# A fused attention and expert-mixture kernel: stores of the last first-layer tiles on another queue, three experts' second-layer weights loaded later, loads and preparations in another order

## The chip, the cores and the metric

The kernel runs on one core of a Trainium2 chip. The metric is the device time of one execution in microseconds (us). TensorE multiplies matrices, VectorE and ScalarE work element by element, GpSimd and SyncE here mostly issue DMAs. Each of ScalarE, SyncE and GpSimd has a DMA queue of its own. An engine takes its instructions strictly in the order of the program, and a DMA issue is such an instruction, waits included. The chip's profiler records one execution; its page calls the engines PE, DVE, ACT, POOL and SP.

## The reference

The first half is attention over 8 batches and 8 heads with 512 local tokens (a window of 32 to each side) and 32 global tokens. Its result, as a matrix `x` of 4352 tokens by 512, feeds a mixture of 8 experts whose routing weights come from 8 rounds of row and column scaling:

```python
logits = x @ w_gate
P = np.exp(logits - logits.max())
for _ in range(8):
    P /= P.sum(1, keepdims=True) + 1e-09
    P /= P.sum(0, keepdims=True) + 1e-09
    P *= N / E
for e in range(E):
    h = np.maximum(x @ w1[e], 0.0)
    out += P[:, e:e + 1] * (h @ w2[e])
```

## The kernel before

**Groups, fillers, units.** The tokens are cut into 9 groups `m`: eight of 512 local tokens and a last one (`m = 8`) of the 256 global tokens. The first layer of experts 0 to 3 needs no routing weight, so it is computed early, as filler work between the steps of the attention: filler (e, m) is `p_l1`, eight tiles `fm` of four matmuls (L466), each followed by a relu (L469 on ScalarE, L471 on VectorE) into a tile `hT`, and after the eighth a store of the whole tile to DRAM (`hd[e][m]`, L473). Fillers run in the order (0,0), (1,0), (2,0), (3,0), (0,1) and so on. The fillers left over when the attention is done are run by `tail_run` (L869), which hands `p_l1` its PSUM pool in the argument `pool`; the fillers within the attention don't set that argument. `tail_run` is called between the steps of the routing rounds (L880 to L888) and once more for all that is left (L901).

**The second stage** runs over 72 units, group by group, with the experts of a group in the order `ORDER = (4, 0, 5, 1, 6, 2, 7, 3)`. Even units are experts 4 to 7: the group's `x` is loaded (`load_x`), scaled by the routing weight (`scale_x`, with the weights `pb` from `load_pb`, which spreads a row of 512 over 128 partitions), and multiplied by first-layer weights `w1s` (`load_w1`, 1 MB; `l1`, L736, relu L738 into `h`). Odd units are experts 0 to 3: their `h` is loaded back from DRAM (`load_h`, L722, 1 MB) and scaled (`scale_h`). Then both go through the second layer as a two-by-two block product with seven products instead of eight (`product`, L779): `sums` makes the sums and differences of blocks of `h`, `prep_w2c` those of the weights `w2c[e]`, five VectorE instructions an expert, once. `add` (L795, L793) brings products from PSUM to the output tile, `store` and, for the last unit, `last_pair` (L819) write it out.

**What sets the order.** The program is scheduled by hand, in the order of the text. Tiles with few buffers tie the engines together: `hT` and `h` share 4 buffers, `w1s` has 2 (the fillers' weights of experts 0 and 1 sit in them first), `pb`, `xs` and `xg` have 2 each, and `ps_rot`, the PSUM tiles of `l1` and of products 6 and 7, has 3. One turn of the loop at L918 does one unit; an even turn `i` holds the first layer of unit `i + 2` among the products of unit `i`, an odd turn has products alone. A pair is an even and an odd turn. SyncE issues, in the order of the program: the stores of fillers; `load_pb(0)`, `load_x(0)`, `load_w1(0)`, `load_pb(1)`, `load_pb(2)` (L890 to L895); the stores of the fillers of L901; `load_w1(2)`, `load_h(1)`; and then in each even turn two `load_pb`, now and then `load_x`, `load_h(i+3)` and `load_w1(i+4)` (L923 to L928). GpSimd issues the second-layer weights, four DMAs an expert (`load_w2c`, L668), which also turn them from 32 to 16 bits: six experts at L682 and the last two, 7 and 3, at L905 to L907, in memory that `xT` has left.

Of the kernel before, what the change touches and what calls it, by code (L numbers as in the profile page):

```python
# [9 lines left out]
FP16 = mybir.dt.float16  # L10
# [13 lines left out]
def kernel(  # L24
# [13 lines left out]
    nc = tc.nc  # L38

    B, H, Sl, Dh = q_l.shape  # L40
# [3 lines left out]
    P = 128  # L44
# [8 lines left out]
    FT = F // P  # L53
# [20 lines left out]
    hd = [[ydram.tile([P, FT, n], FP16, name=f"hd{e}_{m}") for m, (_, n) in enumerate(groups)] for e in range(NL)]  # L74
# [15 lines left out]
    with tc.tile_pool(name="att_c", bufs=1) as att_c, \  # L90
# [131 lines left out]
        for i in range(2):  # L222
            for f, src, eng in zip(f0, (q_l, k_l), (nc.scalar, nc.sync)):
                eng.dma_start(out=f[:, 2 * i : 2 * i + 2].rearrange("p h s d -> p h (s d)"),
                              in_=src[0, 2 * i : 2 * i + 2].rearrange("h (p s) d -> p h (s d)", s=NJ))
# [26 lines left out]
        for so in range(NJ):  # L252
            for c0, n in ((W, P), (W + Sl, W // NJ)):
                nc.vector.tensor_copy(out=zsel[:, so, c0 : c0 + NJ * n].rearrange("p (x s) -> p x s", s=NJ)[:, :, so],
                                      in_=identity[:, 0:n])
# [201 lines left out]
        hTs, wts = {}, {}  # L457

        def p_l1(e, m, fm, eng, pool=None, tag="mm"):
            n = groups[m][1]  # L460
            if fm == 0:
                hTs[(e, m)] = hpool.tile([P, FT, 512], FP16, tag="hT", name="hT")
            hT = hTs[(e, m)]
            ph = (pool or ps_mm).tile([P, 512], FP32, tag=tag, name="ph")
            for dk in range(DP):
                nc.tensor.matmul(ph[:, 0:n], wts[e][:, dk, P * fm : P * (fm + 1)], xT[m][:, dk, :],  # L466
                                 start=(dk == 0), stop=(dk == DP - 1))
            if eng == "a":
                nc.scalar.activation(out=hT[:, fm, 0:n], in_=ph[:, 0:n], func=AF.Relu)  # L469
            else:  # L470
                nc.vector.tensor_scalar(out=hT[:, fm, 0:n], in0=ph[:, 0:n], scalar1=0.0, scalar2=None, op0=ALU.max)  # L471
            if fm == FT - 1:
                nc.sync.dma_start(out=hd[e][m], in_=hT[:, :, 0:n])  # L473

        def load_w1e(e):
            pool, kw = ((wpool, dict(tag="w1e")), (wpool, dict(tag="w1e")), (wpool, dict(tag="w2e", bufs=1)),
# [96 lines left out]
        for s in range(HP, NU + 1):  # L573
            slot = s
            b, hp = divmod(s, HP)
# [84 lines left out]
    ORDER = (4, 0, 5, 1, 6, 2, 7, 3)  # L660
# [4 lines left out]
    def load_w2c(e):  # L665
        w = w2c[e]
        for i, (f, d) in ((1, (0, 0)), (4, (1, 1)), (2, (0, 1)), (3, (1, 0))):
            nc.gpsimd.dma_start(out=w[:, i], in_=moe_w2[e][P * HF * f : P * HF * (f + 1), HD * d : HD * (d + 1)]  # L668
                                .rearrange("(fko fki) d -> fki fko d", fki=P))
# [4 lines left out]
    def prep_w2c(e):  # L674
        w = w2c[e]
        tt(w[:, 0], w[:, 1], w[:, 4], ALU.add)
        tt(w[:, 5], w[:, 1], w[:, 2], ALU.add)
        tt(w[:, 6], w[:, 3], w[:, 4], ALU.add)
        tt(w[:, 2], w[:, 2], w[:, 4], ALU.subtract)
        tt(w[:, 3], w[:, 3], w[:, 1], ALU.subtract)  # L680

    for e in ORDER[:6]:  # L682
        load_w2c(e)

    units = [(m, e) for m in range(B + 1) for e in ORDER]
# [3 lines left out]
    def load_w1(i):  # L689
        if i < NUN:  # L690
            w1s[i] = wpool.tile([P, DP, F], FP16, tag="w1e", name="w1s")
            nc.sync.dma_start(out=w1s[i], in_=w1d[units[i][1] - NL])

    def load_pb(i):
        if i < NUN:
            m, e = units[i]
            c0, n = groups[m]
            pbs[i] = xsp.tile([P, 512], FP32, tag="pb", name="pb")
            nc.sync.dma_start(out=pbs[i][:, 0:n], in_=pd[e, c0 : c0 + n].partition_broadcast(P))
# [6 lines left out]
    def scale_x(i):  # L706
        if i < NUN:
            m = units[i][0]
            n = groups[m][1]
            xss[i] = xsp.tile([P, DP, 512], FP16, tag="xs", name="xs")  # L710
            tt(xss[i][:, :, 0:n], xgs[m][:, :, 0:n],
               pbs.pop(i)[:, 0:n].unsqueeze(1).to_broadcast([P, DP, n]), ALU.mult)
# [17 lines left out]
    def l1(i, fm, pool, tag):  # L730
        if i >= NUN:
            return
        n = groups[units[i][0]][1]
        ph = pool.tile([P, 512], FP32, tag=tag, name="ph")
        for dk in range(DP):
            nc.tensor.matmul(ph[:, 0:n], w1s[i][:, dk, P * fm : P * (fm + 1)], xss[i][:, dk, 0:n],  # L736
                             start=(dk == 0), stop=(dk == DP - 1))
        nc.scalar.activation(out=hs[i][:, fm, 0:n], in_=ph[:, 0:n], func=AF.Relu)  # L738

    def sums(i):  # L740
        if i >= NUN - 1:
            return
        n = groups[units[i][0]][1]
        t1, t2 = slice(0, n // 2), slice(n // 2, n)
        h = hs[i]
        s = ss[i] = (wpool.tile([P, 3, HF, 256], FP16, tag="w2e", name="s", bufs=1) if i % 2 else
                     wr.tile([P, 3, HF, 256], FP16, tag="s", name="s"))
        lo, hi = h[:, 0:HF], h[:, HF:FT]
        tt(s[:, 0:2, :, 0 : n // 2], lo[:, :, 0:n].rearrange("p k (a t) -> p a k t", a=2),
           hi[:, :, 0:n].rearrange("p k (a t) -> p a k t", a=2), ALU.add)  # L750
        tt(s[:, 2, :, 0 : n // 2], lo[:, :, t1], hi[:, :, t2], ALU.add)
        tt(lo[:, :, t2], lo[:, :, t2], lo[:, :, t1], ALU.subtract)
        tt(hi[:, :, t1], hi[:, :, t1], hi[:, :, t2], ALU.subtract)
# [46 lines left out]
    def last_pair(i):  # L800
        m, e = units[i]
        o, h, w = os_[m], hs[i], w2c[e]
        n = groups[m][1]
        lo, hi = h[:, 0:HF, 0:n], h[:, HF:FT, 0:n]
        s = ss[i]
        for c in range(n // P):
            q = slice(P * c, P * (c + 1))
            pm = ps_rot.tile([P, 512], FP32, tag="r", name="pm")
            for d, terms in ((1, ((lo, 2), (s, 4))), (0, ((hi, 3), (s, 1)))):
                for t, (a, wi) in enumerate(terms):  # L810
                    for k in range(HF):
                        nc.tensor.matmul(pm[:, HD * d : HD * (d + 1)], a[:, k, q], w[:, wi, k, :],
                                         start=(d == 1 and t == 0 and k == 0),
                                         stop=(t == 1 and k == HF - 1), skip_group_check=True)
            nc.vector.scalar_tensor_tensor(out=o[:, c, :], in0=pm, scalar=1.0 / float(E), in1=o[:, c, :],
                                           op0=ALU.mult, op1=ALU.add)
            eng = (nc.sync, nc.scalar)[c]
            for b in range(4 * c, 4 * c + 4):
                eng.dma_start(out=out[S * b : S * b + Sg, :], in_=o[W * (b % 4) : W * (b % 4 + 1), c, :])  # L819

    fac = float(E) / float(NTOK)
# [69 lines left out]
    load_x(0)  # L891
    load_w1(0)
    load_pb(1)
    scale_x(0)
    load_pb(2)  # L895
    prep_w2c(4)
    prep_w2c(0)
    scale_x(2)
    prep_w2c(5)
    prep_w2c(1)  # L900
    tail_run(1000)  # L901
    load_w1(2)
    psx.close()
    wr = ctx.enter_context(tc.tile_pool(name="wr", bufs=1, side="right", reuse_waits="tile"))
    for e in ORDER[6:]:  # L905
        w2c[e] = wr.tile([P, 7, FT // 2, D // 2], FP16, name=f"w2c{e}")
        load_w2c(e)  # L907
    alloc_h(0)
    load_h(1)
    for fm in range(FT):  # L910
        pool, tag = cyc[fm % 2]
        l1(0, fm, pool, tag)
    sums(0)
    scale_h(1)
    pss.close()
# [2 lines left out]
    for i, (m, e) in enumerate(units):  # L918
        if i == NUN - 1:
            last_pair(i)  # L920
        elif i % 2 == 0:
            alloc_h(i + 2)
            load_pb(i + 3)  # L923
            load_pb(i + 4)
            if (i + 4) % E == 0:
                load_x((i + 4) // E)
            load_h(i + 3)
            load_w1(i + 4)  # L928
            if i + 2 < NUN:
                sums(i + 1)  # L930
            else:
                n = groups[m][1]
                h = hs[i + 1]
                s = ss[i + 1] = wpool.tile([P, HF, n], FP16, tag="w2e", name="sl", bufs=1)
                tt(s, h[:, 0:HF, 0:n], h[:, HF:FT, 0:n], ALU.add)
            scale_x(i + 4)
            if m == 0:
                for e in {0: (6,), 2: (2, 7), 4: (3,)}.get(i, ()):
                    prep_w2c(e)
            scale_h(i + 3)  # L940
            for fm in range(3):
                l1(i + 2, fm, ps_rot, "r")
            for q, fm in ((3, 3), (4, 4), (5, 5), (2, 6), (1, 7), (6, None), (7, None)):
                product(i, q)
                if fm is not None:
                    l1(i + 2, fm, ps_rot, "r")
            if closes(i):
                for q in (6, 7, 3, 4, 5, 2, 1):
                    add(i, q, fixed[q])
        else:  # L950
            sums(i + 1)
            for q in (6, 7, 3, 4, 5, 2, 1):
                product(i, q)
                if q >= 6 or closes(i):
                    add(i, q, fixed[q])
            if closes(i):
                store(m)
# [31 lines left out]
```

## Time and profile before

| what | us |
|---|---|
| median of 3 runs (1082.46 to 1085.31) | 1083.66 |
| the profiled execution's own time | 1079.91 |
| its span, first to last instruction | 1078.1 |
| attention, fillers and routing rounds: until `lt` is made (L857) | 0 to 373.5 |
| last fillers, and first layer of unit 0 | 373.5 to 414 |
| second stage, 36 pairs (19.13 each in the long middle part) | 414 to 1072.7 |
| last results out | 1072.7 to 1078.1 |
| busy: PE, DVE, ACT, POOL | 1031.6, 809.8, 490.1, 143.0 |

A row of the page's groups or of the timeline gives the start, the time, the engine, the line, the operation, what it writes and from what, how many, and in brackets how long the engine had been idle just before and what ended that. "SPq" is SyncE's queue; the time of such a row runs from the first issue to the end of the last. Granted clock is the share of TensorE's full speed that was granted. In the DMA table, q1 is SyncE's queue, q10 ScalarE's and q0 GpSimd's.

### The profile page before, as it was taken

The numbers are of one execution on the slowest core, as the hardware profiler recorded it, in microseconds if no ns is written. First come the engines' busy times: TensorE is split into PE (matmuls) and PEld (weight loads), VectorE is DVE, ScalarE is ACT, GpSimd is POOL, SyncE is SP. The second block draws the span as 40 slices with busy tenths as digits, with TensorE's granted clock in tenths as the row PEclk, the third lists the DMA queues.
The fourth block names the chain that finished last, engine by engine and source line by source line (L and its number), as shares of the span: only waits on it lengthen the run. The fifth ranks groups of instructions, "written<-read, shape, count | busy, mean of one in ns | idle before, by whom it ended". The sixth has DMA issues, their size and how long they took to land.

```text
span 1078.1 us, 21698 instructions
## 1 busy us (share of the span) xinstructions
PE 1031.6 (96%) x8854; PEld 701.3 (65%) x8854; DVE 809.8 (75%) x1464; ACT 490.1 (45%) x1248; POOL 143.0 (13%) x230
## 2 busy tenths in 40 slices
PE   7899999999999979899999999999999999999988
PEld 4555555555554455667777777777777777777877
DVE  8688777777775656986877877878777678768665
ACT  7777877878875654123222223223223132232221
POOL 7442342332314310000000000000000000000000
PEclk9999999999999989999999999999999999999989
DMA  9977698888939997343624525526416526336251
GB/s 271 232 149 219 145 235 244 163 257 204 176 139 222 262 287 240 118 186 129 223 99 149 208 94 174 193 84 236 154 75 230 205 59 244 147 118 221 69 173 48
DMA packets 113347, 190.82 MB, mean 177 GB/s; under 512 B 33680, under 2 KB 80736, under 8 KB 100448
## 3 DMA queue, kind: packets, MB, share of 16 engines
q1 hardware_dynamic: 63200, 168.00, 44.8%
q0 software_dynamic: 48880, 20.20, 15.4%
q8 instruction: 69, 1.13, 0.4%
q10 hardware_dynamic: 1168, 1.25, 0.4%
q14 instruction: 30, 0.25, 0.1%
HBM read 157.11 MB, written 53.62 MB: 195 GB/s over the span
## 4 chain that ended last, share of the span: by engine, by line
PE 78%; DVE 9%; ACT 7%; DMA 4%; issue 2%; SPq 0%; POOL 0%; ACTq 0%; DVEq 0%
PE m L779 26%; PE ph L736 20%; PE ph L466 14%; PE pm L779 10%; ACT Pu L309 3%; DVE Pu L346 3%; DVE h L672 2%; PE ptw L357 1%; ACT hT L469 1%; ACT qbd L283 1%; PE pt L273 1%; PE pv L155 1%; DMA w1s<-w1d 1%; PE po L378 1%; DMA hd<-hT 1%
## 5 line engine op out<-in xcount | busy, mean ns | idle before, releaser
L738 ACT ACTIVATE h<-ph 128x512 f16<-128x512 f32 (+1 forms) x288 | 164.7, 574 | 420.5 <-PE ph L736 400.9
L736 PE MATMUL ph<-xs,w1s 128*128 128x512 f16 (+1 forms) x1152 | 273.7, 371 | 10.7 <-DMA w1s<-w1d 5.2
L466 PE MATMUL ph<-xT,w1e 128*128 128x512 f16 (+1 forms) x1152 | 257.9, 369 | 6.9 <-ACT hT L469 6.6
L779 PEld LDWEIGHTS <-h 128*128 128x128 f16 x2160 | 212.2, 98 | 45.3 <-issue 0.6
L779 PE MATMUL m<-w2c,s 128*128 128x256 f16 x1620 | 199.9, 273 | 0.0
L672 DVE TENSOR_TENSOR s<-h 128x1024 f16<-128x1024 f16 (+2 forms) x142 | 123.9, 914 | 99.6 <-ACT h L738 53.4
L779 PEld LDWEIGHTS <-s 128*128 128x128 f16 x1620 | 158.6, 98 | 38.3
L736 PEld LDWEIGHTS <-w1s 128*128 128x128 f16 x1152 | 113.9, 99 | 96.2 <-issue 7.7
L466 PEld LDWEIGHTS <-w1e 128*128 128x128 f16 x1152 | 105.9, 98 | 103.4 <-issue 9.8
L672 DVE TENSOR_TENSOR h<-h,pb 128x4096 f16<-128x4096 f16 (+1 forms) x36 | 150.6, 4183 | 3.3 <-DMA h<-hd 2.9
L779 PE MATMUL m<-w2c,h 128*128 128x256 f16 x1080 | 136.9, 275 | 0.0
L469 ACT ACTIVATE hT<-ph 128x512 f16<-128x512 f32 (+1 forms) x191 | 104.4, 558 | 54.7 <-PE ph L466 45.7
L672 DVE TENSOR_TENSOR xs<-xg,pb 128x2048 f16<-128x2048 f16 (+1 forms) x36 | 78.1, 2169 | 61.4 <-DMA pb<-pd 44.5
L779 PE MATMUL pm<-w2c,h 128*128 128x256 f16 x1080 | 123.8, 273 | 0.0
L309 ACT ACTIVATE Pu<-ms,mx 128x160 f16<-128x160 f32 x224 | 93.6, 421 | 3.9 <-DVE mx L306 1.5
L471 DVE TENSOR_SCALAR hT<-ph 128x512 f16<-128x512 f32 x97 | 66.8, 689 | 31.3 <-PE ph L466 30.6
L672 DVE TENSOR_TENSOR h<-h 128x1024 f16<-128x1024 f16 (+1 forms) x142 | 87.6, 659 | 0.0
L306 DVE CUSTOM_DVE_ANT_0 ms<-sc,mask 128x160 f32<-128x160 f32 x224 | 59.9, 320 | 22.8 <-PE sc L301 20.8
L350 POOL TENSOR_TENSOR Pl<-Pu,rs 128x256 f16<-128x256 f16 x32 | 24.6, 768 | 196.6 <-DVE rs L345 131.3
L346 DVE TENSOR_TENSOR Pu<-Pu,rs 128x768 f16<-128x768 f16 x64 | 44.9, 701 | 2.2
L795 DVE SCALAR_TENSOR_TENSOR o<-m,o 128x512 f32<-128x512 f32 (+1 forms) x72 | 43.3, 655 | 4.1 <-ACT o L793 2.3
L309 ACT ACTIVATION_READ_ACCUMULATOR Pu<-ms,mx 128x1 f32 x224 | 42.5, 190 | 0.0
(150 smaller groups left out, 903.5 us busy)
## 6 DMA issues: line engine op xcount, KB each, us to landing
w1s<-w1d SPq DMA_DIRECT2D x36, 1024.0 KB
hd<-hT SPq DMA_DIRECT2D x32, 1024.0 KB
h<-hd SPq DMA_DIRECT2D x32, 1024.0 KB
pb<-pd SPq DMA_DIRECT2D x64, 256.0 KB
w2c<-in_moe_w_dram POOLq DMA_DIRECT2D x32, 256.0 KB, 17.0
out_dram<-o SPq DMA_DIRECT2D x8, 1024.0 KB
f<-in_q_l_dram SPq DMA_DIRECT2D x15, 512.0 KB
f<-in_k_l_dram SPq DMA_DIRECT2D x15, 512.0 KB
```

The lines of the kernel that those rows point to most:

```text
L306: nc.vector.tensor_tensor_reduce(out=ms[:, ii, :], in0=sc[:, SW * ii : SW * (ii + 1)], in1=mask[:, mi, :], scale=-scale, scalar=BIG, op0=A ...
L309: nc.scalar.activation(out=d["Pu"][:, i, :], in_=ms[:, ii, :], func=AF.Exp, scale=-1.0, bias=d["mx"][:, i : i + 1], accum_out=d["sm"][:, i ...
L346: nc.vector.tensor_tensor(out=d["Pu"][:, i0:i1, 0:KW], in0=d["Pu"][:, i0:i1, 0:KW], in1=d["rs"][:, i0:i1].unsqueeze(2).to_broadcast([P, i1 ...
L350: nc.gpsimd.tensor_tensor(out=d["Pl"], in0=d["Pu"][:, :, KW:SW], in1=d["rs"].unsqueeze(2).to_broadcast([P, NHB, Sg]), op=ALU.mult)
L466: nc.tensor.matmul(ph[:, 0:n], wts[e][:, dk, P * fm : P * (fm + 1)], xT[m][:, dk, :], start=(dk == 0), stop=(dk == DP - 1))
L469: nc.scalar.activation(out=hT[:, fm, 0:n], in_=ph[:, 0:n], func=AF.Relu)
L471: nc.vector.tensor_scalar(out=hT[:, fm, 0:n], in0=ph[:, 0:n], scalar1=0.0, scalar2=None, op0=ALU.max)
L672: nc.vector.tensor_tensor(out=out, in0=in0, in1=in1, op=op)
L736: nc.tensor.matmul(ph[:, 0:n], w1s[i][:, dk, P * fm : P * (fm + 1)], xss[i][:, dk, 0:n], start=(dk == 0), stop=(dk == DP - 1))
L738: nc.scalar.activation(out=hs[i][:, fm, 0:n], in_=ph[:, 0:n], func=AF.Relu)
L779: nc.tensor.matmul(pm[:, HD * t : HD * (t + 1)], lhs[0][:, k, lhs[1] + P * t : lhs[1] + P * (t + 1)], w[:, q - 1, k, :], start=(k == 0 and ...
L795: nc.vector.scalar_tensor_tensor(out=o, in0=p, scalar=sg / float(E), in1=o, op0=ALU.mult, op1=ALU.add)
```

## The change

It has five parts. (1) The store at L473 is issued by ScalarE, after its own relu, where `pool` is set, that is, in `tail_run`. (2) Expert 2's second-layer weights are no longer loaded at L682; they, and those of experts 7 and 3, are loaded after a new two-element GpSimd copy, `mark`, that reads the last relu's tile of filler (0,8). (3) The preparations of experts 4, 0 and 5 stand ahead of the first `scale_x`, expert 1's ahead of the second, and expert 6's behind it (it was in turn 0); in the loop, turns 2, 4 and 6 prepare experts 2, 7 and 3, one each. (4) `load_w1` of the even turns is issued one turn earlier, at the head of the odd turn, and the one of turn 0 right behind `l1` of unit 0, ahead of the `load_pb` and `load_h` of the next turn. (5) Of the eight stores of the last unit the fourth goes from GpSimd and the eighth from SyncE; the others stay, three on SyncE and three on ScalarE.

```diff
--- before.py
+++ after.py
@@ -470,7 +470,7 @@
             else:
                 nc.vector.tensor_scalar(out=hT[:, fm, 0:n], in0=ph[:, 0:n], scalar1=0.0, scalar2=None, op0=ALU.max)
             if fm == FT - 1:
-                nc.sync.dma_start(out=hd[e][m], in_=hT[:, :, 0:n])
+                (nc.scalar if pool else nc.sync).dma_start(out=hd[e][m], in_=hT[:, :, 0:n])
 
         def load_w1e(e):
             pool, kw = ((wpool, dict(tag="w1e")), (wpool, dict(tag="w1e")), (wpool, dict(tag="w2e", bufs=1)),
@@ -679,7 +679,7 @@
         tt(w[:, 2], w[:, 2], w[:, 4], ALU.subtract)
         tt(w[:, 3], w[:, 3], w[:, 1], ALU.subtract)
 
-    for e in ORDER[:6]:
+    for e in ORDER[:5]:
         load_w2c(e)
 
     units = [(m, e) for m in range(B + 1) for e in ORDER]
@@ -814,8 +814,8 @@
                                          stop=(t == 1 and k == HF - 1), skip_group_check=True)
             nc.vector.scalar_tensor_tensor(out=o[:, c, :], in0=pm, scalar=1.0 / float(E), in1=o[:, c, :],
                                            op0=ALU.mult, op1=ALU.add)
-            eng = (nc.sync, nc.scalar)[c]
             for b in range(4 * c, 4 * c + 4):
+                eng = {3: nc.gpsimd, 7: nc.sync}.get(b, (nc.sync, nc.scalar)[c])
                 eng.dma_start(out=out[S * b : S * b + Sg, :], in_=o[W * (b % 4) : W * (b % 4 + 1), c, :])
 
     fac = float(E) / float(NTOK)
@@ -891,17 +891,21 @@
     load_x(0)
     load_w1(0)
     load_pb(1)
+    prep_w2c(4)
+    prep_w2c(0)
+    prep_w2c(5)
     scale_x(0)
     load_pb(2)
-    prep_w2c(4)
-    prep_w2c(0)
+    prep_w2c(1)
     scale_x(2)
-    prep_w2c(5)
-    prep_w2c(1)
+    prep_w2c(6)
     tail_run(1000)
     load_w1(2)
     psx.close()
     wr = ctx.enter_context(tc.tile_pool(name="wr", bufs=1, side="right", reuse_waits="tile"))
+    mark = wr.tile([P, 2], FP16, name="mark")
+    nc.gpsimd.tensor_copy(out=mark, in_=hTs[(0, B)][:, FT - 1, 0:2])
+    load_w2c(2)
     for e in ORDER[6:]:
         w2c[e] = wr.tile([P, 7, FT // 2, D // 2], FP16, name=f"w2c{e}")
         load_w2c(e)
@@ -910,6 +914,7 @@
     for fm in range(FT):
         pool, tag = cyc[fm % 2]
         l1(0, fm, pool, tag)
+    load_w1(4)
     sums(0)
     scale_h(1)
     pss.close()
@@ -925,7 +930,6 @@
             if (i + 4) % E == 0:
                 load_x((i + 4) // E)
             load_h(i + 3)
-            load_w1(i + 4)
             if i + 2 < NUN:
                 sums(i + 1)
             else:
@@ -935,7 +939,7 @@
                 tt(s, h[:, 0:HF, 0:n], h[:, HF:FT, 0:n], ALU.add)
             scale_x(i + 4)
             if m == 0:
-                for e in {0: (6,), 2: (2, 7), 4: (3,)}.get(i, ()):
+                for e in {2: (2,), 4: (7,), 6: (3,)}.get(i, ()):
                     prep_w2c(e)
             scale_h(i + 3)
             for fm in range(3):
@@ -948,6 +952,7 @@
                 for q in (6, 7, 3, 4, 5, 2, 1):
                     add(i, q, fixed[q])
         else:
+            load_w1(i + 5)
             sums(i + 1)
             for q in (6, 7, 3, 4, 5, 2, 1):
                 product(i, q)
```

## The prediction

> **What bounds the kernel now.** I read the chain that ended last first, to see which engine sets the end and where it is broken.
>
> ```profile
> PE 78%; DVE 9%; ACT 7%; DMA 4%; issue 2%; SPq 0%; POOL 0%; ACTq 0%; DVEq 0%
> ...
> 375.70 16.96 PE ph L466 x124
> 393.05 7.89 DMA hd<-hT
> 401.48 3.57 PE ph L466 x16
> 405.04 3.47 PE ph L736 x16
> 408.82 7.40 DMA h<-hd
> ...
> 1035.80 8.14 DMA w1s<-w1d
> ```
>
> TensorE sets the time; what can be won are the places where it stands still. TensorE's own timeline has few of them in the second stage, and a long idle is followed by slow matmuls.
>
> ```profile
> 401.48 3.57 PE L466 MATMUL ph<-xT,w1e 128*128 128x256 f16 x16 [6.64 <-ACT hT L469]
> 409.51 3.61 PE L736 MATMUL ph<-xs,w1s 128*128 128x512 f16 x16 [1.02 <-ACT h L738]
> 414.27 2.76 PE L736 MATMUL ph<-xs,w1s 128*128 128x512 f16 x12 [1.14 <-DMA w1s<-w1d]
> 458.04 3.57 PE L736 MATMUL ph<-xs,w1s 128*128 128x512 f16 x8 [4.46 <-DVE o L795]
> 1043.99 2.74 PE L736 MATMUL ph<-xs,w1s 128*128 128x256 f16 x12 [4.07 <-DMA w1s<-w1d]
> ```
>
> At full clock sixteen matmuls of 512 columns take 3.47 on the chain (at 346.63), 0.217 each, and half of that, 0.108, for 256 columns. After the idle of 6.64 sixteen of these take 3.57, twice that; after 1.02 and 1.14 the pace is normal. So the clock falls for an idle somewhere between 1.14 and 4.07. Pairs are 19.13 apart everywhere else, without idle: the change can win at these places only. Why they wait is in the other engines' timelines.
>
> ```profile
> 386.54 6.46 SPq L699 DMA_DIRECT2D pb<-pd  x2
> 393.05 12.96 SPq L473 DMA_DIRECT2D hd<-hT  x5
> 390.36 2.29 DVE L672 TENSOR_TENSOR xs<-xg,pb 128x2048 f16<-128x2048 f16 x1 [16.87 <-DMA xg<-xd]
> 408.87 3.17 ACT L738 ACTIVATE h<-ph 128x512 f16<-128x512 f32 x6 [3.40 <-DMA hd<-hT]
> 444.00 6.10 DVE L672 TENSOR_TENSOR w2c<-w2c 128x1024 f16<-128x1024 f16 x10
> 457.30 1.28 DVE L795 SCALAR_TENSOR_TENSOR o<-pm,o 128x512 f32<-128x512 f32 x2
> 1040.02 1.23 DVE L672 TENSOR_TENSOR xs<-xg,pb 128x1024 f16<-128x1024 f16 x1 [5.58 <-DMA pb<-pd]
> ```
>
> Filler (3,7) is done at 383.3, but its store leaves SyncE only at 393.05, behind `load_pb(2)`, which waits for the first `scale_x`, which waits for `xg`. Filler (3,8) needs that buffer.
>
> **Part 1, the fillers' stores.** On ScalarE the store of (3,7) goes out at 383.5. It took 393.05 to 401.04 (relu released), so it lands by 391.5, before 393.5, where the 25 relus end (10.86 from 382.64) and (3,8) begins. The waits of 7.53 and 6.64 go, and the slow clock (3.57 - 16 x 0.108 = 1.84). TensorE goes on from 394.83: 16 x 0.108 = 1.73, so unit 0 starts at 396.6. Its eight tiles are 4 x 0.2165 each, 6.93 in all: 403.5, where unit 2 could start, against 414.27 now. That is 10.8 at most.
>
> What is late next: unit 0's relus write a buffer that a store of a group-8 filler must have left (the 3.40 at 408.87). Buffers go in the order of last use, taken at first use: now `h` of unit 1, loaded first, takes that of (0,8), and unit 0 that of (1,8), by the semaphores that they wait for. `mark` gives (0,8) a later last use, so I count on (1,8) for unit 1 and (2,8) for unit 0. The four stores leave ScalarE at about 387, 390.6, 394.1 and 397.6 (eight relus are 3.47). Each is 1024 packets of 512 B. What else runs then passes packet for packet, large or small:
>
> ```profile
> q1 hardware_dynamic: 88, 0.72, 88.3%
> q0 software_dynamic: 105, 0.05, 18.4%
> ...
> q1 hardware_dynamic: 626, 0.32, 65.8%
> q0 software_dynamic: 336, 0.17, 60.1%
> ```
>
> These are two windows of 2 us, 390 to 392 (8 KB packets of `w1s` on q1) and 401 to 403 (512 B stores on q1): 44 packets a us beside the weights, 313 beside GpSimd's loads alone. From 387 to 398 SyncE's queue carries `w1s` of unit 0, two `pb` and `w1s` of unit 2, 128 packets each, so about 512 store packets pass. The other 2560 of the first three stores at 313 a us need 8.2: (2,8) lands at 406.2. Unit 0 fills four PSUM tiles to 400.1, waits, goes on 0.64 after the relu (409.51 against 408.87) at 406.8, runs four tiles (3.46) plus 1.8 for the clock: 412.1. **Gain 2.2**. Bounds: 10.8 if no store is waited for; -3.3 if (2,8) lands as late as the last of the four does now, 411.8 by its semaphore. I take 2.2, as the packets are counted in rows.
>
> [...]
>
> Issues cost ScalarE 0.32 to 0.6 each (SyncE's rows: 424 to 601 ns for the first two), in idle of 0.27 a relu and four PSUM tiles of cover: nothing on the path. `mark` is one small copy on an idle GpSimd.
>
> **Part 2, later weights.** Twelve DMAs start at about 387.4 instead of 361.56 to 385.62. In the trace the last twelve took 361.56 to 408, 46 us; so all are there by 434, and the first preparation of them is in turn 2, after 440. Nothing; without that cover the preparation would hold VectorE. Before 387 the DMA engines are freer, so `xg` comes some 5 sooner; unit 0 needs `xs` at 396.6 and had it at 392.65 even now: hidden.
>
> **Part 3, preparations.** Turn 0 loses 3.09 and turn 2 half of 6.10, so 6.1 less stands before the `add` of 457.30. The other half moves to turn 4 and 3.05 to turn 6; those pairs have idle VectorE time (2.33 and 3.00 a pair at 701 and 708), and a lag is carried over two pairs. The `add` comes at 451.2 where TensorE wants its PSUM tile at 453.6, or 451.4 when 2.2 ahead; it ends 0.64 later. The stall cost 463.03 - 436.88 - 19.13 = 7.0 with its slow clock. **Gain 6.5**, bounds 4 (a lag remains) and 7.0.
>
> **Part 4, weights first.** SyncE now stands at `load_w1` until `l1` of two turns before is done, and two `pb` and an `h` wait behind it. From a middle pair: `l1` is done at 700.6, weights out then; `pb` (694.63, 698.96 now) and `h` (702.41) follow. At a group's end SyncE does the same with the output store of 1 MB in front, from 730.15, and `h` is scaled at 740.5, 10.4 later; so here `h` is there at 711.0, and `scale_h` starts at 713.65. Cover 2.6; nothing. At the end the wait for `w1s` at 1043.99 goes, but the `scale_x` beside it ends at 1041.25 for its own `pb`, behind the store of group 7. TensorE stopped at 1039.92, so 1.4 remain, which I take as no slow clock, nearest to 1.14. Idle 4.07 becomes 1.4; turn 66 took 8.61 where turn 64 took 5.68. 2.7 + 2.9 = **gain 5.6**, bounds 2.7 and 7.0.
>
> **Part 5, last stores.** ScalarE's fourth issue (1.77 / 4 = 0.44) goes. SyncE's new one stands where its fourth stood. GpSimd's: a `vg` of 32 KB took 3.5 from issue to landing, so 1073.2 + 3.5 = 1076.7, about where the last lands now. **Gain 0.3**, bounds -0.5 and 0.44.
>
> **Sum:** 2.2 + 6.5 + 5.6 + 0.3 = 14.6 of the profiled 1079.91, its span 1078.1 and 1.8 around it. The runs' median is 3.75 above that; I take the gain off the median: 1083.66 - 14.6 = 1069.1.
>
> **The rivals.** *Stores pass quickly* (no wait for a group-8 store): 10.8 instead of 2.2, so 1060.5. [...] Against: 88 to 105 packets, and the waits of 7.53 and 3.40 on such stores.
>
> *ScalarE is held.* On SyncE the issues of (1,8) and (2,8) took 3.55 and 3.88, as the queue ahead was full; ScalarE would hold its relus as long. Then the first part is -3.3 and VectorE's start is late too (4 of 7.0): 4 + 5.6 + 0.3 - 3.3 = 6.6, so 1077.1. Against: the stores are 3.5 apart and not in one burst.
>
> *The waits only move.* Unit 0 waits as long as now (0), `h` of unit 1, loaded after a store of (1,8), is so late that VectorE's lag stays (0), and of the end only the shorter idle is won (2.7): 1083.66 - 2.7 = 1081.0. For it: `h` of unit 1 took 408.82 to 416.2 on the chain, and `scale_h` follows it at 417.04. Against: (1,8) lands 3.3 before (2,8), at 403, and 7.4 more is 410.
>
> *Slower: weights ahead of `h`.* The place is SyncE's queue in each of some 33 pairs. If `h` lands later than 713.65, every pair slips by the excess; it decides against the change from 14.6 / 33 = 0.44 a pair, a landing 3.0 later than I work out. With 1.0 a pair: 1069.1 + 33 = 1102. For it: `h` was waited for 7 times (2.9 in all) even now. Against: the 2.6 of cover and VectorE's idle time.
>
> **How the numbers follow.** Forecast 0.62 (1065 to 1075), quick stores 0.17, ScalarE held 0.12, wait moved 0.05, slower 0.04. Runs of one kernel spread by 0.3%, about 3.2, which is what can be told from no change. Faster: 0.62 + 0.17 + 0.12 = 0.91; same 0.05; slower 0.04. The range 1060 to 1077 holds the forecast, the better part of the quick stores and of the held ScalarE.
>
> **What would show it.** Right: no idle at the last filler; unit 0's relus wait for `hd<-hT` until about 406; no 4.46 before the first layer in turn 4; 1.4 for `xs` at turn 66; pairs still 19.13 apart. Wrong: pairs longer than 19.13, a `DMA_DIRECT2D` of 3 us on ScalarE's queue, `scale_h` waiting for `hd`.

## The result, and the profile after

The changed kernel took 1076.14 us (median of 6 runs, 1073.39 to 1077.14) where the kernel before took 1083.91 (6 runs, 1081.35 to 1088.65): a ratio of 0.9922, 95% interval 0.9898 to 0.9946. It is faster, by about 8 us where 14.6 were forecast. The profiled execution took 1073.39, its span 1071.6 (before 1078.1).

TensorE's timeline, in the places that were shown of before:

```profile
397.61 1.91 PE L466 MATMUL ph<-xT,w1e 128*128 128x256 f16 x16 [2.14 <-ACT hT L469]
399.35 3.62 PE L736 MATMUL ph<-xs,w1s 128*128 128x512 f16 x16
411.49 8.44 PE L736 MATMUL ph<-xs,w1s 128*128 128x512 f16 x28 [8.52 <-ACT h L738]
...
456.75 1.89 PE L736 MATMUL ph<-xs,w1s 128*128 128x512 f16 x8 [0.28 <-DVE o L795]
...
1038.42 1.47 PE L736 MATMUL ph<-xs,w1s 128*128 128x256 f16 x12 [2.19 <-DVE xs L672]
...
1050.20 1.03 PE L736 MATMUL ph<-xs,w1s 128*128 128x256 f16 x8 [1.46 <-DVE o L795]
```

The last filler's idle fell from 6.64 to 2.14 and its slow clock is gone, but unit 0 now stands still for 8.52 in its middle, where it stood for 1.02, and runs on at a slow clock: 28 matmuls take 8.44, at 0.217 each they would take 6.1. The idle at turn 4 is nearly gone (4.46 to 0.28). At turn 66 it fell from 4.07 to 2.19, and turn 68 has a new one of 1.46.

The other engines at these places:

```profile
384.17 2.29 DVE L672 TENSOR_TENSOR xs<-xg,pb 128x2048 f16<-128x2048 f16 x1 [1.03 <-DMA xg<-xd]
394.17 2.90 ACTq L473 DMA_DIRECT2D hd<-hT  x1
397.17 2.76 ACT L469 ACTIVATE hT<-ph 128x256 f16<-128x256 f32 x8 [3.03 <-issue]
399.96 1.45 ACTq L473 DMA_DIRECT2D hd<-hT  x1
410.84 2.06 ACT L738 ACTIVATE h<-ph 128x512 f16<-128x512 f32 x4 [10.90 <-DMA hd<-hT]
...
456.01 1.28 DVE L795 SCALAR_TENSOR_TENSOR o<-pm,o 128x512 f32<-128x512 f32 x2
...
1037.05 1.23 DVE L672 TENSOR_TENSOR xs<-xg,pb 128x1024 f16<-128x1024 f16 x1 [5.94 <-DMA pb<-pd]
```

The first scaling is 6.2 earlier, and unit 0 has its `xs` long before it needs it. ScalarE stood 2.90 and 1.45 at the issues of (2,8) and (3,8), where an undisturbed one takes 0.33. Unit 0's relus then waited 10.90 for a store; by the semaphores it is (2,8), landed at 410.76, and so unit 0 has the buffer that was worked out.

The chain of waits can't be read as before. The last results leave on GpSimd's queue too, the chain is followed back along that engine, which had done nothing since the weights, and it ends in 655.97 of "issue":

```profile
issue 64%; PE 20%; ACT 6%; DVE 5%; DMA 3%; POOL 1%; ACTq 0%; POOLq 0%
```

So the span is cut at points on TensorE that every version has. *Transition*: from the first matmul into `pt` (L862) to the first one into `pm` (L779) of turn 0. *Turn 2 to 4*: between the first `pm` matmuls of these turns, 19.13 when undisturbed. *End*: from the first `pm` of turn 62 to the end of the span. Between turns 8 and 62 lie 513.19 in every kernel here. Ahead of the transition lie 371.92 to 378.17 in different executions, though the program is nearly the same there; TensorE's granted clock in the first 50 us differs too (0.97 in the changed kernel's execution, 0.93 in version 3's). One span is therefore no measure, and the stretches are.

| kernel | median | ratio to before, 95% | transition | turn 2 to 4 | end |
|---|---|---|---|---|---|
| before | 1083.91 | | 52.01 | 26.15 | 55.82 |
| changed | 1076.14 | 0.9922 (0.9898 to 0.9946) | 54.28 | 19.57 | 53.01 |
| 1 all stores on SyncE | 1080.70 | 0.9986 (0.9972 to 1.0001) | 60.47 | 19.13 | 52.84 |
| 2 copy reads `xs` | 1077.48 | 0.9960 (0.9943 to 0.9977) | 58.43 | 19.13 | 52.36 |
| 3 loads after unit 0's relu | 1062.91 | 0.9824 (0.9803 to 0.9846) | 41.47 | 19.90 | 52.32 |
| 4 stores without gaps | 1064.35 | 0.9837 (0.9815 to 0.9858) | 44.98 | 19.88 | 52.85 |
| 5 preparations as before | 1084.13 | 1.0020 (1.0003 to 1.0038) | 54.31 | 27.43 | 52.73 |
| 6 `load_w1` as before | 1076.53 | 0.9954 (0.9939 to 0.9970) | 54.62 | 19.13 | 54.79 |
| 7 loads as before | 1073.76 | 0.9931 (0.9910 to 0.9953) | 52.55 | 19.13 | 52.08 |
| 8 = 3, all stores on SyncE | 1065.95 | 0.9855 (0.9833 to 0.9877) | 44.16 | 19.75 | 51.92 |
| 9 = 3, `pb` a turn earlier | 1066.97 | 0.9860 (0.9835 to 0.9885) | 41.62 | 20.02 | 56.38 |
| 10 = 9, no gaps | 1066.05 | 0.9843 (0.9818 to 0.9867) | 41.06 | 20.58 | 56.03 |
| 11 = 3, output store on GpSimd | 1060.47 | 0.9798 (0.9772 to 0.9824) | 41.54 | 19.89 | 48.85 |
| 12 = 11, no gaps | 1058.85 | 0.9786 (0.9764 to 0.9808) | 41.06 | 20.24 | 48.90 |

A ratio is to executions of the kernel before that ran beside the version; their medians lie between 1081.62 and 1083.91, so medians of different rows compare versions less well than the ratios and the stretches do. Between the changed kernel and version 3, for instance, the medians differ by 13.2, the ratios by about 10.6 us.

The changed kernel's gain of 6.5 between the two spans is thus -0.6 ahead of the transition (chance), -2.3 in it, +6.6 at turn 4 and +2.8 at the end.

### The profile page after: what moved, and what is told of

It is laid out like the page before. It is cut to its first block, busy times and chain, and to the rows that moved or that the text cites. A ratio compares the mean times of both kernels' runs of the same rounds, so it can differ in the third digit from the quotient of the medians.

```text
span 1071.6 us, 21704 instructions
## 1 busy us (share of the span) xinstructions
PE 1026.9 (96%) x8854; PEld 698.8 (65%) x8854; DVE 808.8 (75%) x1464; ACT 489.2 (46%) x1248; POOL 144.0 (13%) x232
## 4 chain that ended last, share of the span: by engine, by line
issue 64%; PE 20%; ACT 6%; DVE 5%; DMA 3%; POOL 1%; ACTq 0%; POOLq 0%
PE ph L466 14%; ACT Pu L309 3%; DVE Pu L346 2%; DMA w2c<-in_moe_w_dram 2%; PE ptw L357 1%; ACT hT L469 1%; ACT qbd L283 1%; PE pt L273 1%; DMA f<-in_k_l_dram 1%; PE po L378 1%; PE sc L299 1%; DVE m L409 1%; PE pt L426 1%; ACT Pg L412 1%; PE po L381 0%
## 5 line engine op out<-in xcount | busy, mean ns | idle before, releaser
L779 PEld LDWEIGHTS <-h 128*128 128x128 f16 x2160 | 211.3, 98 | 44.3
L779 PE MATMUL m<-w2c,s 128*128 128x256 f16 x1620 | 199.9, 273 | 0.0
L779 PEld LDWEIGHTS <-s 128*128 128x128 f16 x1620 | 158.5, 98 | 38.4 <-DVE s L672 0.2
L779 PE MATMUL m<-w2c,h 128*128 128x256 f16 x1080 | 135.2, 273 | 0.0
L779 PE MATMUL pm<-w2c,h 128*128 128x256 f16 x1080 | 123.8, 273 | 0.0
```

Source lines behind the costliest of these rows:

```text
L779: nc.tensor.matmul(pm[:, HD * t : HD * (t + 1)], lhs[0][:, k, lhs[1] + P * t : lhs[1] + P * (t + 1)], w[:, q - 1, k, :], start=(k == 0 and ...
```

## Experiments on the transition

**1. All fillers' stores on SyncE's queue again.**

```
-  (nc.scalar if pool else nc.sync).dma_start(out=hd[e][m], in_=hT[:, :, 0:n])
+  nc.sync.dma_start(out=hd[e][m], in_=hT[:, :, 0:n])
```

> The changed kernel with all fillers' stores on SyncE's queue again; everything else as changed. Theory (landing decides: unit 0's relus wait for the store whose buffer unit 0 takes, and a store of 1024 packets of 512 B is slow on whichever queue it is): filler (3,7)'s store leaves SyncE at about 386.6, once the first scaling has let go of a pb buffer, so filler (3,8) still starts by 395.5; the stores of (1,8) and (2,8) land within 2 us of 405.6 and 410.8; the time is within 3 us of the changed kernel's. Rival (ScalarE held at issue decides): no relu of (3,8) is held, TensorE's idle of 2.14 there goes, unit 0's relus come 2.9 earlier or more, and the time is 3 us or more below the changed kernel's. What the prediction's first term says by itself (stores on ScalarE save 2.2): 2 us above the changed kernel's.

The transition is 6.2 longer than in the changed kernel. (1,8) landed at 405.54 and (2,8) at 410.43, as the theory says (counted from the start of the transition, 2.2 and 1.9 later than in the changed kernel), but SyncE stood 4.41 and 3.91 at their issues, and what comes behind them on that queue was late. The buffers changed as well: by the semaphores unit 0 takes that of (1,8) here, and its first relu runs at 405.65. TensorE's timeline:

```profile
396.40 3.48 PE L466 MATMUL ph<-xT,w1e 128*128 128x256 f16 x16 [3.19 <-ACT hT L469]
...
406.30 5.30 PE L736 MATMUL ph<-xs,w1s 128*128 128x512 f16 x16 [2.87 <-ACT h L738]
418.48 5.30 PE L736 MATMUL ph<-xs,w1s 128*128 128x512 f16 x12 [6.88 <-DMA w1s<-w1d]
```

The issue of unit 2's weights, behind the four stores, began only at 401.64 and took 4.66; they landed at 418.43, and TensorE waited 6.88 for them. So neither theory had the size right. The holding of ScalarE is not what decides: here ScalarE is never held, and the kernel is slower. ScalarE's queue, with the buffers that go with it, is worth 6.2 in the changed kernel, and the largest wait of this version is for weights that stood behind the stores on SyncE.

**2. Another buffer for unit 0.** In the changed kernel the small copy on GpSimd gives (0,8) a later use, and unit 0 takes (2,8)'s buffer. Here it reads `xs`, ready at nearly the same time.

```
-  nc.gpsimd.tensor_copy(out=mark, in_=hTs[(0, B)][:, FT - 1, 0:2])
+  nc.gpsimd.tensor_copy(out=mark, in_=xss[0][:, 0, 0:2])
```

> The changed kernel, but the small GpSimd copy reads the first scaled activations (ready at 386.5) and not filler (0,8)'s tile, so that the twelve loads behind it start within 1 us of the same time while filler (0,8)'s buffer keeps its earlier last use. Theory (the buffer that unit 0 takes decides): unit 1 takes the buffer of (0,8) again and unit 0 that of (1,8), whose store lands at 405.6 and not at 410.8; unit 0's relus start at about 405.7, TensorE's idle there is 3.4 and not 8.52, and the time is 4 to 5 us below the changed kernel's. Rival (ScalarE held at issue decides): the relus and their idle stay as they are, within 1 us of the changed kernel's time.

The transition became 4.2 longer: both were wrong on the time. TensorE's and ScalarE's timelines:

```profile
408.38 6.20 PE L736 MATMUL ph<-xs,w1s 128*128 128x512 f16 x28 [1.97 <-ACT h L738]
423.78 1.87 PE L736 MATMUL ph<-xs,w1s 128*128 128x512 f16 x4 [8.33 <-ACT h L738]
...
407.73 3.17 ACT L738 ACTIVATE h<-ph 128x512 f16<-128x512 f32 x6 [4.89 <-DMA hd<-hT]
...
423.14 1.58 ACT L738 ACTIVATE h<-ph 128x512 f16<-128x512 f32 x3 [10.51 <-DMA hd<-hT]
```

Unit 0 did take (1,8)'s buffer (landed 407.65), and its idle fell from 8.52 to 1.97. Then unit 2 waited 8.33 for the buffer of the last store, (3,8), landed at 423.05. In the changed kernel (3,8) landed at 417.81 and unit 2's first relu ran at 418.24: its wait was hidden, with 0.4 to spare, behind unit 0's. Four buffers wait for four stores, and here another order of the buffers moved the wait from unit 0 to unit 2 and didn't shorten it.

**3. The moved loads after the stores.** The copy reads unit 0's `h`, and the twelve loads of part 2 come behind it (both are gone from their old place, which isn't shown here).

```
     for fm in range(FT):
         l1(0, fm, pool, tag)
+        if fm == 0:
+            nc.gpsimd.tensor_copy(out=mark, in_=hs[0][:, 0, 0:2])
+            for e in (2, *ORDER[6:]):
+                load_w2c(e)
```

> As the kernel before this one in the call, but the small copy reads the first tile of unit 0's h, so that GpSimd's twelve loads start only once unit 0's first relu has run. Theory (GpSimd's loads share the DMA engines packet for packet with the stores and make them late): the stores of (0,8) and (1,8) have only SyncE's weights beside them; (1,8) lands by 402, unit 0's relus start by then, and the time is 7 to 9 us below the changed kernel's; the loads are there by 445, early enough for turn 2. Rival (SyncE's 8 KB weights alone make the stores late): (1,8) lands at 405 as with the other copy, and the time is that kernel's within 1 us.

The transition lost 12.8 and the median 13.2: more than the theory gave. TensorE ran through:

```profile
399.44 1.91 PE L466 MATMUL ph<-xT,w1e 128*128 128x256 f16 x16 [0.24 <-ACT hT L469]
401.19 9.66 PE L736 MATMUL ph<-xs,w1s 128*128 128x512 f16 x44
```

All 44 matmuls of unit 0 and of unit 2's start follow each other at 0.217. The reason stands in the packets by queue. First the changed kernel from 400 to 410, then this one from 402 to 405 (q0 GpSimd's queue, q10 ScalarE's, q1 SyncE's; packets, MB, share of the 16 DMA engines' time, which passes 100% where the records of packets overlap):

```profile
q0 software_dynamic: 2145, 1.07, 77.1%
q10 hardware_dynamic: 2142, 1.08, 52.7%
q1 hardware_dynamic: 4, 0.03, 0.8%
```

```profile
q10 hardware_dynamic: 2064, 1.04, 114.9%
```

Beside the loads the stores pass at 214 packets a us, one for one; alone at 688. The stores landed at 402.02, 403.53, 405.45 and 409.00, and the last of the loads at 439.15, ahead of their preparations. One more thing differs from the changed kernel: by the semaphores unit 0 takes the buffer of (1,8) again. Version 2 has these buffers too, with the loads in the changed kernel's place, and its transition is 17.0 longer; so the gain comes from the loads and not from the buffers.

**4. Fewer packets.** The tiles of the last group are written without gaps, so a store is 128 packets of 4 KB and not 1024 of 512 B; the bytes, the queues and the loads are the changed kernel's (the small copy reads the same values at their new place).

```
-  hT = hTs[(e, m)]
+  hT = hTs[(e, m)].rearrange("p f n -> p (f n)")[:, 0 : FT * n].rearrange("p (f n) -> p f n", f=FT)
```

> The changed kernel, but the fillers of the last group (256 columns) are written without gaps in their buffer, so that each store is 128 packets of 4 KB and not 1024 of 512 B; buffers, queues and the small copy as changed. Theory (packets are passed one for one, so the number of a store's packets decides): (2,8)'s store lands within 4 us of its issue, by 402; neither ScalarE's issues (2.90 and 1.45) nor unit 0's relus are held, the idles of 2.14 and 8.52 go with the slow clock, and the time is 9 to 12 us below the changed kernel's. Rival (bytes decide: the same 512 KB pass beside the same loads): (2,8) lands within 2 us of 410.8 and the time is within 2 us of the changed kernel's.

The transition lost 9.3 and the time 11.8. ScalarE's issue of (2,8), and TensorE:

```profile
398.17 0.33 ACTq L473 DMA_DIRECT2D hd<-hT  x1
...
406.74 7.89 PE L736 MATMUL ph<-xs,w1s 128*128 128x512 f16 x28 [2.08 <-ACT h L738]
```

From 392 to 408 ScalarE's queue passed 576 packets with 2.10 MB, where the changed kernel's passed 2142 with 1.08 MB from 400 to 410. No issue was held, and (2,8) landed 7.8 after it and not 16.6, but not within the 4 expected; unit 0 still waits 2.08. The same bytes in an eighth of the packets thus win most of what 3 wins, with unit 0 still in (2,8)'s buffer (landed 406.01), which shows that the stores' count of packets beside the loads is the greater part of the price.

**7. Loads where they were.**

```
-    for e in ORDER[:5]:
+    for e in ORDER[:6]:
         load_w2c(e)
...
-    mark = wr.tile([P, 2], FP16, name="mark")
-    nc.gpsimd.tensor_copy(out=mark, in_=hTs[(0, B)][:, FT - 1, 0:2])
-    load_w2c(2)
```

> The changed kernel with the w2c loads of experts 2, 7 and 3 at the places of the kernel before, without the small copy that holds them back (four of them go with the first loads, eight as soon as their memory is free); stores stay on ScalarE's queue. What the prediction says of this part: nothing, within 1 us of the changed kernel's time. Theory now (the twelve loads held until the stores of the last group are under way are what make those stores, and h and weights behind them, late): part of the loads are done before the stores start, the last store lands 3 to 6 us earlier counted from its issue, and the time is 3 to 8 us below the changed kernel's.

The theory fell: the ratio can't be told from the changed kernel's, and the transition is 1.7 shorter. Now the loads run earlier, and still seven of them land between 399.90 and 420.22, while the four stores, issued from 390.39 on, land between 407.39 and 421.39. Without the copy unit 0 also takes the buffer of (1,8), as in version 2, so the 1.7 is not the loads' place alone. ScalarE's queue and TensorE:

```profile
397.39 6.60 ACTq L473 DMA_DIRECT2D hd<-hT  x1
...
404.52 3.57 PE L466 MATMUL ph<-xT,w1e 128*128 128x256 f16 x16 [5.84 <-ACT hT L469]
```

Here the holding of ScalarE does reach TensorE: 6.60 at one issue, 5.84 of idle. The place that the change gave the loads is as bad as the old one; only one behind the stores is good.

**8. SyncE's queue, with the loads behind.** Version 3 with the edit of 1.

> The twelve w2c loads held until unit 0's first relu has run (as in the earlier kernel, 1062.9 us), and all fillers' stores on SyncE's queue. Theory (ScalarE's queue still matters once the loads are out of the way, since SyncE's store of (3,7) waits behind a pb load, and the loads of w1s and h wait behind four stores): 3 to 6 us above that kernel, 1066 to 1069. Rival (with GpSimd's loads away the queue of the stores is worth nothing): within 1.5 us of it.

2.7 more in the transition and 3.0 in the median, at the lower end of the theory; the buffers are those of 3. ScalarE's queue is worth this much without the loads, less than with them.

## Experiments on the loop and the end

**5. Preparations in the turns of before.**

```
     scale_x(2)
-    prep_w2c(6)
     tail_run(1000)
...
-                for e in {2: (2,), 4: (7,), 6: (3,)}.get(i, ()):
+                for e in {0: (6,), 2: (2, 7), 4: (3,)}.get(i, ()):
```

> The changed kernel with the preparations of experts 6, 2, 7 and 3 in the turns of the kernel before (6 in turn 0, 2 and 7 in turn 2, 3 in turn 4) instead of one ahead of the loop and one each in turns 2, 4, 6. Theory (the prediction's third term): the add on VectorE is late again, TensorE's idle at turn 4 is about 4.5 and not 0.28, with slow matmuls behind it, and the time is 6 to 7 us above the changed kernel's. Rival (the lag that the changed kernel removes would now be hidden, since the transition leaves VectorE 16 us idle ahead of turn 0): the time is within 2 us of the changed kernel's.

```profile
447.68 6.10 DVE L672 TENSOR_TENSOR w2c<-w2c 128x1024 f16<-128x1024 f16 x10
...
460.98 1.28 DVE L795 SCALAR_TENSOR_TENSOR o<-pm,o 128x512 f32<-128x512 f32 x2
...
461.71 3.57 PE L736 MATMUL ph<-xs,w1s 128*128 128x512 f16 x8 [5.47 <-DVE o L795]
```

The ten additions are in turn 2 again, the add is late, and the stretch is 7.9 longer than the changed kernel's. The third term stands, though the idle of 5.47 is longer than the 4.5 expected.

**6. `load_w1` behind `h`, as before.**

```
-    load_w1(4)
     sums(0)
...
             load_h(i + 3)
+            load_w1(i + 4)
...
         else:
-            load_w1(i + 5)
             sums(i + 1)
```

> The changed kernel with each turn's weights loaded after that turn's h, as before the change. Theory (of what the end gave, 4.7 came at turn 66 and 1.6 went back at turn 68, where VectorE's add is late behind the scaling that waits for pb): TensorE's idle of about 4 on w1s comes back at turn 66 with slow matmuls, the idle at turn 68 goes, and the time is 2.5 to 4 us above the changed kernel's. Rival (the idle at turn 68 does not hang on turn 66): both are there, and the time is 5 to 7 us above.

```profile
1041.61 2.08 PE L736 MATMUL ph<-xs,w1s 128*128 128x256 f16 x12 [4.05 <-DMA w1s<-w1d]
```

The wait on `w1s` is back, and it is the only idle at the end: turn 68 has none. The idle there does hang on turn 66. From `pm` to `pm`, turn 66 took 15.50 (before 16.78, changed 12.07) and turn 68 9.61 (changed 11.23). The end is 1.8 longer, and the median, 0.4 higher, lies below the 2.5 to 4 expected (by the ratios it is about 3.5). Twelve matmuls took 2.08 after this idle of 4.05, and 2.74 after the 4.07 of before the change: the clock stayed low for a shorter time here.

**9. `pb` ahead of the output store.** In version 3, each turn's two `pb` loads leave a turn earlier.

```
     scale_h(1)
+    load_pb(3)
+    load_pb(4)
...
             alloc_h(i + 2)
-            load_pb(i + 3)
-            load_pb(i + 4)
...
         else:
+            load_pb(i + 4)
+            load_pb(i + 5)
             load_w1(i + 5)
```

> The kernel with the twelve w2c loads held until unit 0's first relu (1062.9 us), and each turn's two pb loads issued one turn earlier on SyncE, so that at the end they go ahead of the 1 MB store of the last full group. Theory (the store holds pb back, pb holds the scaling, the scaling holds TensorE 1.36 at turn 66, and VectorE's lateness is carried to turn 68): the idle on xs goes and the one on o at turn 68 shrinks by half at least; from the first product of turn 62 to the end it is 2 to 3 us less, 49.3 to 50.3 in place of 52.3; 1060 to 1061. Rival (h, not pb, sets VectorE at the end: its load waits for the same store and for buffers): the idle on xs goes and the one on o at turn 68 stays; at most 1.4 less.

Both were wrong: the end is 4.1 longer. The idle on `xs` went, and a larger one came at turn 68. SyncE's queue and TensorE:

```profile
1020.60 6.44 SPq L699 DMA_DIRECT2D pb<-pd  x2
1027.13 0.38 SPq L692 DMA_DIRECT2D w1s<-w1d  x1
1027.60 0.53 SPq L722 DMA_DIRECT2D h<-hd  x1
...
1039.68 1.87 PE L736 MATMUL ph<-xs,w1s 128*128 128x256 f16 x8 [4.72 <-DVE o L795]
```

The second `pb` of the next turn stood until 1026.72 for its buffer; the weights and `h` were queued behind it, `h` landed at 1035.37, and VectorE, which scales `h` ahead of the add, was late.

**10. The last group's `h` without gaps too.** Version 9, with the view of 4 on the fillers' tiles and on the `h` tiles as well.

> As the kernel before it in the call, and the h tiles of the last group (256 columns) without gaps in their buffer, for the fillers' stores and for the loads in the last turns, so that each store and load is 128 packets of 4 KB and not 1024 of 512 B. Theory (the count of packets decides in the last turns too): the loads of h there land about 2 us sooner after their issue, VectorE waits no more for h, the idle on o at turn 68 goes; 1 to 2 us below the kernel before it. Rival (the loads are late by their issue, which waits for buffers, and not by their packets): within 0.7 us of it.

The end is 0.35 shorter, which speaks for the rival, and the idle at turn 68 is still there (4.38). The median is 0.9 lower, between what the two give, and the intervals overlap. `h` landed 7.7 after its issue (7.8 in 9); the weights were issued just ahead of it on the same queue and landed 1.2 before it, which may be why fewer packets didn't help.

**11. The output store on GpSimd's queue.** Version 3 with one word changed in `store`.

```
-  nc.sync.dma_start(out=out[S * m + Sg : S * (m + 1)]...
+  nc.gpsimd.dma_start(out=out[S * m + Sg : S * (m + 1)]...
```

> The kernel with the twelve w2c loads held until unit 0's first relu (1062.9 us), and the 1 MB store of each full group from GpSimd's queue and not SyncE's; the pb loads stay where they were. Theory (in the last turns pb, and h and pb behind it on SyncE's queue, are late by the store ahead of them in that queue): pb of turn 64 lands 2 us or more sooner after its issue, the idle on xs at turn 66 (1.36) goes, the next pb and h are issued 2 us sooner and the idle on o at turn 68 (1.65) shrinks; the stretch from the first product of turn 62 to the end falls from 52.3 to 49.5 to 51; 1060 to 1062. Rival (the waits only move, as when pb went ahead of the store: an h load behind weights is late next): the stretch is 52 to 56 and the time is not below 1062.

SyncE's and GpSimd's queue:

```profile
1010.72 0.86 SPq L699 DMA_DIRECT2D pb<-pd  x2
1012.09 0.53 SPq L722 DMA_DIRECT2D h<-hd  x1
1023.84 0.32 SPq L692 DMA_DIRECT2D w1s<-w1d  x1
...
1020.95 0.75 POOL L798 DMA_DIRECT2D out_dram<-o  x1 [72.37 <-DVE o L795]
```

The end fell by 3.5 to 48.85, and TensorE has no idle left there. The gain is larger than expected because the store's bytes were not the point. Its issue waits for VectorE's last add, and on SyncE the `pb` of turn 64 waited with it: in version 3 to 1020.91, here it left at 1010.72, with the two executions 0.3 apart at turn 0.

**12. The same without gaps.** Version 11, with both views of 10.

> As the kernel before it in the call, with the h tiles of the last group without gaps, in stores and loads (128 packets of 4 KB). Theory (with the loads of w2c out of the way and the store off SyncE's queue, the count of packets matters no more): within 1 us of the kernel before it, the transition within 0.7 of 41.5. Rival (packets still count at the end): 1 to 3 us below it.

The transition is 0.5 shorter and the end the same, as the theory said; the median is 1.6 lower, as the rival said, but the intervals overlap, so this isn't decided by the times. By the ratios versions 11 and 12 are about 2% below the kernel before and 1.2 to 1.4% below the changed one.

## Why the prediction was partly wrong

*Part 1, the fillers' stores: mis-sized.* Right: (3,7)'s store left at 383.90 and landed at 388.29, the wait for it is gone, and unit 0 takes (2,8)'s buffer. Wrong is the step "at 313 a us need 8.2: (2,8) lands at 406.2". The stores ran beside GpSimd's loads at 214 a us, as counted above, and (2,8) landed at 410.76, near the worse of the two bounds. The 313 came from a window of 2 us in which ScalarE's queue was empty and the other two carried 481 a us; here all three together carry 429. That window's own counts, 626 and 336, are not one for one either: three of GpSimd's loads were still on their way in it (they landed at 403.12, 405.70 and 408.05), while in the changed kernel eight were at 400. This fits the lower rate and wasn't tested by itself. Ahead of 398 the count erred the other way: 896 store packets had passed by then where 512 were taken. The term, 2.2, came out at -2.3, within its bounds of -3.3 and 10.8. A second wait was not worked out: unit 2 needs the buffer of (3,8), so that a punctual (2,8) alone would have won little (version 2). And "issues cost ScalarE 0.32 to 0.6 each ... nothing on the path" was wrong: one issue took 2.90, and an idle of 2.14 came of it.

*Part 2, later weights: "nothing" was right against the kernel before, and missed the point.* Against the old place the new one is worth -1.7 in the transition by version 7 (whose buffers differ too), too little to tell in the times. But in both places the loads run beside the stores, and this costs 12.8 in the changed kernel's transition (version 3). I asked of the twelve loads only whether they arrive in time, not what they do to the stores around them.

*Part 3, preparations: right in the cause and the size, not in the margin.* 6.5 forecast; the stretch is 6.6 shorter. But the `add` was worked out to end 1.7 before TensorE wants its tile, and it held TensorE for 0.28: in turn 0 the scaling that waits for `pb` ran 2.41 after the turn's first `pm`, and 0.81 after it before the change, so VectorE made up less than was counted on.

*Part 4, the end: mis-sized.* The idle on `xs` was worked out as 1.4 and is 2.19, with no slow clock, as taken. The prediction set TensorE's stop of before the change against the `xs` of before the change; both moved. TensorE came to it 3.69 earlier than before and `xs` only 2.97. Turn 66 gave 4.7 of the 5.6. Then 1.6 went back at turn 68, where VectorE, started late by the same `pb`, ended the add late: the question of what is late next was not asked a second time. 5.6 became 3.1. The middle was right: 513.19 between turns 8 and 62 in both kernels, so *weights ahead of h* did not come.

*Part 5: wrong in sign.* From the first `pm` of the last pair to the end of the span it is 9.78 before and 10.06 after: -0.3 where +0.3 was taken, within the bounds. The last issue ended 0.35 earlier after that matmul (6.93 and not 7.28), but the last store landed 0.15 later (8.78 and not 8.63); why is not tested.

*The rivals.* *ScalarE is held* gave 1077.1, and the time is within 1 us of it. The held issue is in the trace, at 2.90, but its sum isn't: it added 4.0, 5.6, 0.3 and -3.3, and the runs gave 6.6, 3.1, -0.3 and -2.3, so that the nearness of the time is luck. That a full queue holds the issue was an inference: the runs show 2.90 at the third store of 1024 pieces and 0.33 at one of 128 (version 4). And the transition's loss comes from where the stores landed: in version 1 ScalarE is not held at all, and the transition is longer still. *Stores pass quickly* fell with the wait of 10.90, and no run shows stores of 1024 packets that pass quickly beside GpSimd's loads: 214 packets a us passed beside them in the changed kernel and 688 alone in version 3. The prediction's "packet for packet, large or small" is more than its two windows can tell, with 88 to 105 at 390 and 626 to 336 at 401; near-equal counts, 2142 and 2145, were seen where both queues carried packets of some 500 B, in the changed kernel from 400 to 410.

## What to carry to other kernels

When loads are moved, count their packets beside those of every transfer that something waits for, and work the landing out with the loads in the window (here 214 store packets a us beside them and 688 alone); being on time themselves says nothing of what they delay. A tile that was stored with gaps cost as many packets here as it had pieces, 1024 of 512 B where one without gaps cost 128 of 4 KB: closing the gaps is an edit of one line. And an issue that waits for a late result belongs on a queue on which nothing else is awaited (the end was 3.5 shorter in version 11); after each wait that is removed, ask twice what is late next.

## What the runs showed of the hardware

At its issue of the third store of 1024 pieces, with the two before it not yet landed, ScalarE was held for 2.74, 2.90, 3.21, 3.97 and 6.60 where GpSimd's loads ran beside them (version 5, the changed kernel, versions 6, 2 and 7), for 1.00 without these loads (version 3), and for 0.33 at the same store of 128 pieces, with the loads (version 4).

TensorE's clock by stretches of 4 us (busy time and instructions of PE, PEld, DVE, ACT and POOL, then the granted clock, the DMA share and GB/s): first the changed kernel during and after the idle of 8.52, then version 6 after one of 2.44 that ended at 399.34:

```profile
404.00:408.00 4.00, 0.00 (x0) 0.00 (x0) 0.00 (x0) 0.00 (x0) 0.78 (x2) 0.73 1.30 215
408.00:412.00 4.00, 0.51 (x2) 0.24 (x2) 0.00 (x0) 1.16 (x3) 0.74 (x1) 0.50 1.22 313
```

```profile
400.00:404.00 4.00, 4.00 (x18) 2.10 (x16) 3.57 (x6) 1.55 (x5) 0.75 (x1) 0.58 1.29 220
```

The length of the idle alone does not decide. Idles of 2.14 and 2.19 in the changed kernel had no slow matmuls behind them; one of 2.08 had (version 4, 28 matmuls in 7.89 where 6.1 is the full pace), and so had the one of 2.44 (version 6, 16 matmuls in 2.37, which took 1.91 in the changed kernel). So the prediction's reading, a fall for an idle somewhere between 1.14 and 4.07, has no single threshold behind it in these runs.
